# A third chunk's decays loaded earlier, and two more products ahead of the second pair's outputs, in a planned Mamba-2 plus expert-mixture kernel

## The chip, the cores and the metric

The kernel runs on one core of a Trainium2 chip. The metric is the device time of one execution in microseconds (us). Three executions of the kernel before took 616.87, 616.92 and 619.2 us, so its median is 616.92 us. The profile is of one execution, taken by the hardware profiler. Engine names follow the profile: PE is TensorE (matmul), PEld its weight load, DVE is VectorE, ACT is ScalarE, POOL is GpSimd, SP is SyncE, which here issues nearly all DMAs.

## The reference

The input is a state-space block followed by a mixture of four expert networks. There are 4 sequences of 768 positions, 8 heads, head size 32, state size 16.

```
# state space block, per batch and head, in chunks
L = exp(cum_i - cum_j), kept where i >= j       # cum: running sum of log(clip(a, 1e-6, 1))
y = ((C B^T) * L) x  +  C state * exp(cum)
state = exp(sum) * state + sum_j B_j x_j exp(cum_last - cum_j)
# bridge: x = y as [3072, 256]
# mixture of experts, e = 0..3, F = 1024
p = domain_probs / (row sum + 1e-9)
out += p[:, e] * (relu(x @ w1[e]) @ w2[e])
```

## The kernel before

The 3072 positions are cut into 24 chunks of 128; four chunks with the same place in their sequences follow one another. For each pair of chunks the kernel makes scores (L502, function `score`), multiplies them with a decay matrix into the tile MT on DVE (L856), and then makes the outputs of the pair and what they add to the state on PE (L546, function `inner`; with L879 for the share of the state of an earlier chunk, from the fifth chunk on). ACT copies the outputs away (L894) and keeps the state's part (L556).

For the first six chunks the decay matrix is made by scans on DVE (L519) into the tile LT. Chunks 0 to 2 get the decays spread over partitions by PE; from chunk 3 on they come from DRAM as a broadcast load (`load_decays`, L463) into one of two tiles `ab`. That load reads `acut_d`, a DRAM copy of the clipped decays with each first entry zeroed, which the kernel itself stores (`store_decays`, L630) after POOL has clipped the decays `a_sb` in place (L608), copied them (L626) and zeroed the first column (L627).

The expert networks take the products with the weights (L933, function `product`: one product is two matmuls of 128x256, and the trace has two records for each such matmul). Most of the work is done in schemes that save products by sums of blocks (L1024 for weights, L960, L1043 and L1260 for tokens and results). The first pair of chunks is done with plain products, four blocks of w1 (`plain_first`) and eight products for the second layer (`own_`, from `visit`); each second-layer product needs one gated result of DVE (L968) and one block of w2. The second pair begins with the products named `begun` and `ones`.

Two things set the order around the change. The first stage, up to about 13 us, is written out by hand in the order of the text: the loads on SP are issued in that order, by one sequencer that waits in place. Everything after it is a list of pieces of work. PE's order is the list `line`, written by hand; for DVE, ACT, POOL and SP a planner (`Plan.run`) simulates the engines with given costs and times at which tiles are ready (`plan.taken(..., now + x)`) and fixes their order before the kernel runs. The constants OWN, SCORED and LEFT say how many second-layer products of the first pair stand ahead of the second pair's outputs, ahead of the third pair's scores, and behind the third pair's outputs:

```
line.extend(own_[:OWN])
outputs([2, 3])
...
fill = own_[OWN:SCORED] + put(*[begun[two][0] for two in twos]) + ones + own_[SCORED:]
line.extend(fill[:SCORED - OWN])
scores([4, 5])
line.extend(fill[SCORED - OWN:len(fill) - LEFT])
outputs([4, 5])
line.extend(fill[len(fill) - LEFT:])
```

The names "second pair" and "third pair" below are chunks 2 and 3, and chunks 4 and 5.

Of the kernel before, what the change touches and what calls it, by code (L numbers as in the profile page):

```python
# [10 lines left out]
ALU = mybir.AluOpType  # L11
# [22 lines left out]
LEAN = 4.0  # L34
EASY = 40.0
SCANNED = 6
SCORED, OWN, LEAD, LEFT = 5, 2, 5, 3
FILLED = 3
HORIZON, OPENING, LOADED = 26.0, 80.0, 1.0
ORDERS = (0, 1, 2, 3), (3, 1, 2, 0), (0, 1, 2, 3), (3, 1, 2, 0)  # L40
# [319 lines left out]
def kernel(  # L360
# [10 lines left out]
    nc = tc.nc  # L371

    NCH, _, W = xbc.shape
# [19 lines left out]
    def real(c):  # L393
        return c % NSEQ * NC + c // NSEQ
# [5 lines left out]
    def turned(c):  # L400

        lo = P // NQ * turn_of(c) if c >= NSEQ else 0
        return [(lo, 0, P - lo), (0, P - lo, lo)][:1 + (lo > 0)]
# [17 lines left out]
    def some(n, shape, name, pool=const):  # L421
        return [pool.tile(shape, FP32, name=f"{name}{i}") for i in range(n)]

    homes = {
        "V": some(NV - 4, [P, 2, FB], "v"),
        "W": some(NW, [P, 2 * FB], "w"),
        "bank": some(8, [P, 512], "bank", psum),
        "xb": some(4, [P, W], "xb"),
        "ab": some(2, [P, NH * P], "ab"),
        "ah": some(3, [HN, P], "ah"),  # L430
        "MT": some(2, [P, 2, NH, P + N], "MT"),
        "ctm": some(4, [HN, NT, P], "ctm"),
# [14 lines left out]
    st = {c: {} for c in range(NCH)}  # L447
# [4 lines left out]
    def load_tokens(c, xb):  # L452
        src = xbc[real(c)]
        if len(turned(c)) > 1:
            nc.sync.dma_start(out=xb[:, :OBT], in_=src[:, :OBT])
            for there, here, n in turned(c):
                nc.sync.dma_start(out=xb[here:here + n, OBT:], in_=src[there:there + n, OBT:])
        else:
            nc.sync.dma_start(out=xb, in_=src)

    def load_decays(c, ab):
        src = acut_d if c < SCANNED else cum_d
        nc.sync.dma_start(  # L463
            out=ab, in_=src[real(c)].rearrange("h s -> (h s)").partition_broadcast(P))
# [10 lines left out]
    def load_w1(fb, w):  # L475
        e, f = divmod(fb, EPB)
        nc.sync.dma_start(
            out=w.rearrange("p (a f) -> p a f", a=2),
            in_=w1[e].rearrange("(a p) f -> p a f", a=2)[:, :, f * FB:f * FB + FB])

    def load_w2(fb, w):
        e, f = divmod(fb, EPB)
        nc.sync.dma_start(
            out=w.rearrange("p (j m) -> p j m", j=JJ),
            in_=w2[e, f * FB:f * FB + FB].rearrange("(j p) m -> p j m", p=P))
# [27 lines left out]
    def place(c, h):  # L513

        return (h + NH // 2) % NH if c >= NSEQ and c % 2 else h

    def scan(LT, src, lo):
        w = src.shape[1]
        nc.vector.tensor_tensor_scan(  # L519
            out=LT.rearrange("p h s -> p (h s)")[:, lo:lo + w], data0=src,  # L520
            data1=ident.rearrange("p h s -> p (h s)")[:, :w], initial=0.0,
            op0=ALU.mult, op1=ALU.add)

    def decay(c, MT, ab, neg, h):

        nc.scalar.activation(  # L526
            out=MT[:, place(c, h), 0:P], in_=ab[:, h * P:h * P + P], func=AF.Exp,
            bias=neg[:, h % NT, NQ * real(c) + h // NT:NQ * real(c) + h // NT + 1])
# [22 lines left out]
    def keep_state(c, A, y):  # L551
# [14 lines left out]
    a_sb = homes["cum"][0]  # L566
    a_cut = homes["V"][-4][:NCH * NH // 2, 0].rearrange("p (r s) -> p r s", r=2)
# [5 lines left out]
        out=aq0.rearrange("(q r) t s -> q r (t s)", q=NQ)[:, 0], in_=a_rows[:, 0])  # L573
    nc.scalar.dma_start(
        out=aq1.rearrange("(q r) c t s -> q r c (t s)", q=NQ)[:, 0], in_=a_rows[:, 1:SPREAD])
# [5 lines left out]
        out=a_sb, in_=a.rearrange("c h s -> (c h) s").rearrange("(p r) s -> p r s", r=2))  # L581
# [14 lines left out]
    for q in range(NQ):  # L596
        nc.vector.memset(tmask[32 * q:32 * q + N, 0:1], 1.0)
    nc.vector.tensor_scalar(out=tmask[:, 1:2], in0=tmask[:, 0:1], scalar1=-1.0, scalar2=1.0,
                            op0=ALU.mult, op1=ALU.add)
# [7 lines left out]
    def clip(engine, v, top=1.0):  # L607
        engine.tensor_scalar(out=v, in0=v, scalar1=1e-6, scalar2=top, op0=ALU.max, op1=ALU.min)  # L608
# [13 lines left out]
    clip(nc.vector, aq1.rearrange("p c t s -> p (c t s)"), own)  # L622
    nc.vector.memset(aq1[:, :, :, 0:1], 0.0)

    clip(nc.gpsimd, a_sb)
    nc.gpsimd.tensor_copy(a_cut, a_sb)  # L626
    nc.gpsimd.memset(a_cut[:, :, 0:1], 0.0)  # L627

    def store_decays(engine, d, sb):
        engine.dma_start(  # L630
            out=d.rearrange("c h s -> (c h) s").rearrange("(p r) s -> p r s", r=2), in_=sb)

    store_decays(nc.sync, acut_d, a_cut)
    load_tokens(3, xb[3])
    for fb in range(2, 4):
        load_w1(fb, homes["W"][fb])
    for fb in range(4):
        load_w2(fb, homes["W"][4 + fb])
    load_decays(3, homes["ab"][0])

    BANK = homes["bank"]
    rows = NCH * E
# [22 lines left out]
    def scan_quarters(c, LT, banks, part):  # L665
        for q in (2 * part, 2 * part + 1):
            scan(LT, banks[q][:, :NT * P], q * NT * P)
# [56 lines left out]
    for r in range(2):  # L724
        nc.vector.tensor_tensor_scan(
            out=sums[:, r], data0=a_sb[:, r], data1=zeros[:NCH * NH // 2], initial=0.0,
            op0=ALU.add, op1=ALU.add)
# [14 lines left out]
    plan = Plan(homes)  # L742
    line = []
    B512, B256 = {"DVE": D512, "POOL": 1.3}, {"DVE": D256, "POOL": .72}
    now = 13.2
# [9 lines left out]
    def act(us, fn, **kw):  # L755
        return plan.add({"ACT": us}, fn, **kw)

    def dve(us, fn, **kw):
        return plan.add({"DVE": us}, fn, **kw)
# [4 lines left out]
    def value(kind, **kw):  # L764
        return Value(kind, **kw)
# [8 lines left out]
    for c, i in ((2, 2), (3, 3)):  # L774
        st[c]["xb"] = plan.taken("xb", i, now)
    st[2]["ctm"] = plan.taken("ctm", 0, now)
    st[3]["ab"] = plan.taken("ab", 0, now + 2)
    for c in range(2):
        st[c]["A"] = plan.taken("A", c, now)
    g0 = gates[0, 0] = plan.taken("gate", 0, now)  # L780
# [18 lines left out]
    def decays(c):  # L799
        s = st[c]  # L800
        j = c % 2
        if not j:
            s["MT"] = st[c + 1]["MT"] = value("MT")
            s["made"] = st[c + 1]["made"] = []
        if c < SCANNED:
            for part in range(2):
                if c < SPREAD:
                    dve(1.2, lambda e, part=part: scan_quarters(
                        c, LT0[:, j], [b.t for b in s["a"]], part),
                        reads=s["a"][2 * part:2 * part + 2], part=LTv[2 * j:2 * j + 2])  # L810
                else:
                    half = NH * P // 2
                    dve(1.15, lambda e, lo=half * part: scan(
                        LT0[:, j], s["ab"].t[:, lo:lo + half], place(c, lo // P) * P), two=True,
                        reads=[s["ab"]], part=LTv[2 * j:2 * j + 2])
            plan.add({"POOL": .4}, lambda e: fade(
                c, s["MT"].t[:, j], s["xb"].t, LT0[:, j]),
                reads=[s["xb"], *LTv[2 * j:2 * j + 2]], part=[s["MT"]])
        else:
            made = {}  # L820
            for h in range(NH):
                made[h] = act(.38, lambda e, h=h: decay(
                    c, s["MT"].t[:, j], s["ab"].t, neg.t, h),
                    reads=[s["ab"], neg], part=[s["MT"]])
            cut = [plan.add({"POOL": .85}, lambda e, h=h: causal(
                s["MT"].t[:, j], place(c, h), NQ), part=[s["MT"]],
                behind=[made[x] for x in range(h, h + NQ)]) for h in range(0, NH, NQ)]
            s["made"] += cut
            if c < NCH - NSEQ:
                s["made"].append(plan.add({"POOL": .5 if place(c, 0) else .4}, lambda e: fade(  # L830
                    c, s["MT"].t[:, j], s["xb"].t, s["MT"].t[:, j]),
                    reads=[s["xb"]], part=[s["MT"]], behind=cut))
        if "ctm" not in s:
            s["ctm"] = value("ctm")
            act(.62, lambda e: mask(c, s["ctm"].t, s["xb"].t), reads=[s["xb"]], writes=[s["ctm"]])
        if c >= NSEQ:
            s["dec"], s["cts"] = value("dec"), value("cts")
            act(.3, lambda e: nc.scalar.activation(out=s["dec"].t, in_=s["ah"].t, func=AF.Exp),
                reads=[s["ah"]], writes=[s["dec"]])
            plan.add({"POOL": .72}, lambda e: nc.gpsimd.tensor_mul(  # L840
                s["cts"].t, s["ctm"].t, s["dec"].t.unsqueeze(1).to_broadcast([HN, NT, P])),
                reads=[s["ctm"], s["dec"]], writes=[s["cts"]])
# [503 lines left out]

    loaded = {}
    for fb in range(4):
        loaded[fb, 1] = plan.taken("W", fb, now + (0.0 if fb < 2 else 3.0))
        loaded[fb, 2] = plan.taken("W", 4 + fb, now + 4.0 + fb)  # L1350
    for (fb, l), v in loaded.items():
        weights["S", fb, l] = v

# [31 lines left out]
    for seq, _ in plain[2:]:  # L1385
        line.extend(seq)
    dma(lambda _: nc.sync.dma_start(
        out=g0.t[:, 4:6], in_=p_d[0, 4:6].rearrange("c s -> (c s)").partition_broadcast(P).rearrange(
            "p (c s) -> p c s", s=P)), kb=128, part=[g0])
# [7 lines left out]
    for c in (4, 5):  # L1397
        fetch(c)
        decays(c)
# [11 lines left out]
    made = [twos_first(two, begun[two]) for two in twos]  # L1411
# [48 lines left out]
    for u, (k, fbs) in enumerate(units):  # L1460
# [6 lines left out]
        seq, h = fours_first(k, fbs)  # L1467
# [96 lines left out]
```

## Time and profile before

| what | us |
|---|---|
| median of three executions | 616.92 (616.87 to 619.2) |
| span of the profiled execution, first to last instruction | 615.3 |
| PE busy | 605.7 (98%) |
| DVE busy | 489.5 (80%) |
| ACT busy | 292.5 (48%) |
| POOL busy | 157.6 (26%) |
| PE share of the chain that ended last | 92% |
| mean granted clock of PE | 0.997 |

For the profiled execution the span is what is given; against the median of the executions, 1.6 us (616.92 less 615.3) lie around it. The busy time of PE says how much of the span its records cover, not that each record ran at its best: a matmul of 128x256 has a record of 381 ns on average, while in a dense stretch, 24 records from 18.17 to 23.62 us, one starts every 0.227 us. Times within the span are counted from its start.

### The profile page before, as it was taken

How to read it: one execution, taken by the hardware profiler on the slowest of the kernel's cores; microseconds unless marked ns; L12 is line 12 of the kernel's file. 1: busy time of each engine (PE TensorE's matmuls, PEld its weight loads, DVE VectorE, ACT ScalarE, POOL GpSimd, SP SyncE). 2: the span in 40 equal slices, each digit the busy share in tenths (PEclk: the TensorE clock that was granted, in tenths of full speed). 3: DMA queues.
4: the chain of work that ended last, by engine and by line, in shares of the span. 5: the costliest groups of instructions: out<-in, count | busy, mean ns of one | idle time of the engine just before them, and what ended most of it. 6: DMA issues, size and time to landing. Idle time of an engine off the chain costs nothing.

```text
span 615.3 us, 10136 instructions
## 1 busy us (share of the span) xinstructions
PE 605.7 (98%) x3365; PEld 514.8 (84%) x3365; DVE 489.5 (80%) x854; ACT 292.5 (48%) x681; POOL 157.6 (26%) x238
## 2 busy tenths in 40 slices
PE   9899999999999999999999999999999999999997
PEld 5677878888888888888888888888888888888885
DVE  7879897998969895697978988386785979576775
ACT  4237646378651327877443333844444242434441
POOL 5536556636372000776500100210000000000000
PEclk9899999999999999999999999999999999999999
DMA  7737578676863429983442424964233232964001
GB/s 249 256 114 231 204 218 300 205 224 208 280 188 94 134 34 285 297 291 146 132 144 77 137 63 118 284 222 137 61 111 87 93 90 51 303 230 126 1 0 52
DMA packets 89060, 99.65 MB, mean 162 GB/s; under 512 B 27428, under 2 KB 58928, under 8 KB 89008
## 3 DMA queue, kind: packets, MB, share of 16 engines
q1 hardware_dynamic: 88852, 98.95, 51.4%
q8 instruction: 27, 0.44, 0.3%
q14 instruction: 25, 0.20, 0.1%
q10 hardware_dynamic: 156, 0.06, 0.0%
HBM read 78.80 MB, written 20.17 MB: 161 GB/s over the span
## 4 chain that ended last, share of the span: by engine, by line
PE 92%; DVE 2%; ACT 1%; issue 0%; DVEq 0%
PE bank L933 88%; PE bank L546 2%; PE bank L502 1%; PE bank L879 1%; DVE v L960 1%; DVE v L968 1%; ACT A L556 1%; DVE MT L856 0%; ACT v L894 0%; DVE bank L1071 0%; DVE v L1260 0%; PE bank L1325 0%; DVE v L1425 0%; ACT LT L894 0%; ACT v L1330 0%
## 5 line engine op out<-in xcount | busy, mean ns | idle before, releaser
L933 PE MATMUL bank<-v,w 128*128 128x256 f32 x1716 | 402.0, 381 | 1.1 <-DVE bank L1071 0.8
L933 PEld LDWEIGHTS bank<-v,w 128*128 128x128 f32 x1716 | 325.7, 191 | 50.0 <-issue 2.9
L933 PE MATMUL bank<-Y,w 128*128 128x256 f32 x692 | 177.3, 381 | 0.7 <-ACT LT L894 0.4
L933 PEld LDWEIGHTS bank<-Y,w 128*128 128x128 f32 x692 | 130.2, 190 | 21.9 <-issue 1.7
L1213 ACT COPY v<-bank 128x512 f32<-128x512 f32 x109 | 63.9, 586 | 177.5 <-PE bank L933 165.2
L968 DVE SCALAR_TENSOR_TENSOR v<-bank,gate 128x512 f32<-128x512 f32 x147 | 101.0, 688 | 39.6 <-PE bank L933 36.8
L960 DVE TENSOR_TENSOR v<-v,v 128x512 f32<-128x512 f32 x179 | 125.9, 720 | 2.1 <-ACT v L942 0.8
L1024 POOL TENSOR_TENSOR w<-w,w 128x256 f32<-128x256 f32 x94 | 72.1, 784 | 46.0 <-DVE v L960 13.8
L1071 DVE TENSOR_TENSOR bank<-bank,v 128x512 f32<-128x512 f32 x81 | 55.5, 696 | 35.2 <-PE bank L933 23.6
L942 ACT COPY v<-bank 128x512 f32<-128x512 f32 x97 | 56.7, 587 | 55.0 <-PE bank L933 46.7
L947 ACT COPY bank<-v 128x512 f32<-128x512 f32 x126 | 73.2, 594 | 10.8 <-DVE v L968 8.7
L526 ACT ACTIVATE MT<-ab,neg 128x128 f32<-128x128 f32 x144 | 46.9, 393 | 2.0 <-DMA ab<-cum_d 2.0
L933 PE MATMUL bank<-LT,w 128*128 128x256 f32 x168 | 42.6, 380 | 0.0
L531 POOL TENSOR_SCALAR_AFFINE_SELECT MT<-MT 128x512 f32<-128x512 f32 x36 | 23.0, 652 | 67.8 <-ACT MT L526 53.9
L933 PEld LDWEIGHTS bank<-LT,w 128*128 128x128 f32 x168 | 31.8, 190 | 4.6 <-DVE v L968 0.3
L1024 POOL TENSOR_TENSOR w<-w 128x256 f32<-128x256 f32 x32 | 24.2, 762 | 23.2 <-DVE Y L1043 9.0
L960 DVE TENSOR_TENSOR v<-bank,v 128x512 f32<-128x512 f32 x26 | 17.9, 689 | 11.7 <-PE bank L933 9.9
L1260 DVE TENSOR_TENSOR v<-v,v 128x256 f32<-128x256 f32 x58 | 22.9, 431 | 1.1 <-ACT v L1213 0.7
L856 DVE TENSOR_TENSOR MT<-bank,MT 128x512 f32<-128x512 f32 x36 | 22.7, 681 | 0.1
L968 DVE SCALAR_TENSOR_TENSOR v<-v,gate 128x512 f32<-128x512 f32 x26 | 19.7, 758 | 0.4
L1213 ACT COPY LT<-bank 128x512 f32<-128x512 f32 x12 | 7.0, 586 | 23.5 <-PE bank L933 23.5
L840 POOL TENSOR_TENSOR cts<-ctm,dec 128x256 f32<-128x256 f32 x20 | 14.5, 734 | 11.6 <-DVE v L960 5.1
(110 smaller groups left out, 322.1 us busy)
## 6 DMA issues: line engine op xcount, KB each, us to landing
w<-w_d SPq DMA_DIRECT2D x128, 256.0 KB
w_d<-w SPq DMA_DIRECT2D x64, 256.0 KB
w<-in_w_dram SPq DMA_DIRECT2D x40, 256.0 KB
ab<-cum_d SPq DMA_DIRECT2D x18, 512.0 KB
w<-in_w_dram SPq DMA_DIRECT2D x64, 128.0 KB
gate<-p_d SPq DMA_DIRECT2D x15, 384.0 KB
xb<-in_xbc_dram SPq DMA_DIRECT2D x17, 192.0 KB
out_dram<-v SPq DMA_DIRECT2D x144, 16.0 KB
```

Source lines behind the costliest of these rows:

```text
L526: nc.scalar.activation(out=MT[:, place(c, h), 0:P], in_=ab[:, h * P:h * P + P], func=AF.Exp, bias=neg[:, h % NT, NQ * real(c) + h // NT:NQ ...
L531: nc.gpsimd.affine_select(out=MT[:, h:h + n, 0:P], in_=MT[:, h:h + n, 0:P], compare_op=ALU.is_ge, fill=0.0, base=0, pattern=[[0, n], [1, P ...
L856: nc.vector.tensor_mul(to, g, LT0[:, js, h] if cs[0] < SCANNED else to)
L933: nc.tensor.matmul(out=o, lhsT=w[:, j], rhs=x if half is None else x[:, j], start=(start and j == 0), stop=(j == 1), skip_group_check=True)
L942: act(.5, lambda e: nc.scalar.copy(out=flat(v), in_=bank.t), reads=[bank], writes=[v])
L947: act(.54 if to - lo > FB else .32, lambda e: nc.scalar.copy(out=bank.t[:, lo:to], in_=flat(v)[:, lo:to]), reads=[v], writes=[bank])
L960: plan.add(engines, lambda e: (on(e).tensor_add if sign > 0 else on(e).tensor_sub)(flat(v), whole(x), whole(y)), reads=[x, y], writes=[v], ...
L968: dve(D512, lambda e: nc.vector.scalar_tensor_tensor(out=h.t, in0=whole(x).rearrange("p (j m) -> p j m", j=JJ), scalar=0.0, in1=g.t[:, 2 * ...
L1024: plan.add(B256, lambda e, r=r, x=x, y=y, sign=sign: (on(e).tensor_add if sign > 0 else on(e).tensor_sub)(view(r), view(x), view(y)), two= ...
L1071: dve(D512, lambda e: (nc.vector.tensor_add if sign > 0 else nc.vector.tensor_sub)(to.t, bank.t, whole(x)), reads=[x, bank], writes=[to])
L1213: act(.5, lambda e: nc.scalar.copy(out=flat(v), in_=bank.t), reads=[bank], writes=[v], hold=HOLD)
L1260: plan.add(engines, lambda e: (on(e).tensor_add if sign > 0 else on(e).tensor_sub)(o[1](), x[1](), y[1]()), reads=[v for v in vs if v is n ...
```

## The change

The decays' DRAM copy is made on another engine and stored a little earlier in the text: DVE clips `a_sb` straight into `a_cut` and zeroes its first column, and POOL clips `a_sb` in place after that, where it had clipped, copied and zeroed. The load of chunk 3's decays is issued ahead of the two w1 and four w2 loads instead of behind them. OWN goes from 2 to 4 and SCORED from 5 to 7 (LEFT stays 3). Three ready times and one cost that the planner reckons with are altered.

```diff
-SCORED, OWN, LEAD, LEFT = 5, 2, 5, 3
+SCORED, OWN, LEAD, LEFT = 7, 4, 5, 3
...
+    nc.vector.tensor_scalar(out=a_cut, in0=a_sb, scalar1=1e-6, scalar2=1.0, op0=ALU.max, op1=ALU.min)
+    nc.vector.memset(a_cut[:, :, 0:1], 0.0)
     clip(nc.gpsimd, a_sb)
-    nc.gpsimd.tensor_copy(a_cut, a_sb)
-    nc.gpsimd.memset(a_cut[:, :, 0:1], 0.0)
...
     store_decays(nc.sync, acut_d, a_cut)
     load_tokens(3, xb[3])
+    load_decays(3, homes["ab"][0])
     for fb in range(2, 4):
         load_w1(fb, homes["W"][fb])
     for fb in range(4):
         load_w2(fb, homes["W"][4 + fb])
-    load_decays(3, homes["ab"][0])
...
-    st[3]["ab"] = plan.taken("ab", 0, now + 2)
+    st[3]["ab"] = plan.taken("ab", 0, now + 2.5)
...
-                made[h] = act(.38, lambda e, h=h: decay(
+                made[h] = act(.30, lambda e, h=h: decay(
...
-        loaded[fb, 1] = plan.taken("W", fb, now + (0.0 if fb < 2 else 3.0))
-        loaded[fb, 2] = plan.taken("W", 4 + fb, now + 4.0 + fb)
+        loaded[fb, 1] = plan.taken("W", fb, now + (0.0 if fb < 2 else 4.0))
+        loaded[fb, 2] = plan.taken("W", 4 + fb, now + 6.0 + .8 * fb)
```

With LEFT at 3, what stands behind the third pair's outputs changes too. Before, three second-layer products of the first pair stood there; after, the two products `ones` and one of the first pair. Ahead of the second pair's outputs, between them and the third pair's scores, and between those scores and the third pair's outputs stood 2, 3 and 6 products; after the change it is 4, 3 and 4. On DVE the four MT products of the third pair follow each other, where two gated results had stood between them.

## The prediction

> **What bounds the kernel now.** I read the page first. PE is busy for 98% of the span and holds 92% of the chain that ended last, nearly all of it in the dense products L933. So time can only be won where PE stands still or runs slowly. PE's list of waits, longest first, tells where:
>
> ```profile
> PE 605.7 (98%) x3365; PEld 514.8 (84%) x3365; DVE 489.5 (80%) x854; ACT 292.5 (48%) x681; POOL 157.6 (26%) x238
> PEclk9899999999999999999999999999999999999999
> ...
> PE bank L546 <- POOL w L1024: 1.4, 1, 1.4
> PE bank L684 <- PEq L1556: 0.8, 1, 0.8
> PE bank L933 <- DVE bank L1071: 0.8, 1, 0.8
> PE bank L1325 <- DVE v L1260: 0.7, 1, 0.7
> PE bank L546 <- DVE MT L856: 0.7, 1, 0.7
> ```
>
> Two of the waits are at L546, the outputs of the second pair, and in the page's second slice of the clock an 8 stands: the only dip inside the span. PE's timeline and the table by stage show both:
>
> ```profile
> 18.17 5.45 PE L933 MATMUL bank<-v,w 128*128 128x256 f32 x24
> 24.98 0.41 PE L546 MATMUL bank<-MT,xb 128*32 128x144 f32 x2 [1.36 <-POOL w L1024]
> 26.08 1.18 PE L546 MATMUL bank<-MT,xb 128*32 128x144 f32 x30 [0.70 <-DVE MT L856]
> 27.19 4.54 PE L933 MATMUL bank<-v,w 128*128 128x256 f32 x12
> ...
> 25.38:27.39 2.01, 1.31 (x32) 1.00 0.87 273
> 27.39:30.80 3.41, 3.41 (x9) 0.50 0.60 228
> 30.80:38.50 7.70, 7.70 (x52) 1.00 0.11 39
> ```
>
> The reader is to see that 24 records of L933 take 5.45 us ahead of the wait (0.227 each), but 12 take 4.47 us behind it (chain: 27.26 to 31.73, 0.37 each): the column after the counts is the granted clock, and it is 0.50 from 27.39 to 30.80. The first wait is put down to POOL; by the chain of waits it was DVE, whose MT products ended at 24.83 and 26.04. So the third view is DVE's timeline:
>
> ```profile
> 16.56 0.67 DVE L968 SCALAR_TENSOR_TENSOR v<-bank,gate 128x512 f32<-128x512 f32 x1
> 19.13 1.23 DVE L519 TENSOR_TENSOR_SCAN LT<-ab,ident 128x512 f32<-128x512 f32 x1 [1.90 <-DMA ab<-acut_d]
> 20.27 0.67 DVE L968 SCALAR_TENSOR_TENSOR v<-bank,gate 128x512 f32<-128x512 f32 x1
> 20.85 1.39 DVE L519 TENSOR_TENSOR_SCAN LT<-ab,ident 128x512 f32<-128x512 f32 x1
> 25.34 0.68 DVE L856 TENSOR_TENSOR MT<-bank,LT 128x512 f32<-128x512 f32 x1
> ```
>
> DVE waits 1.90 us for chunk 3's decays and then works without a break until MT is done at 26.02.
>
> **What the stall costs.** PE ends its products at 23.62 and the outputs at 27.26: 3.64 us for 32 matmuls that take 1.12 us in the third pair (39.12 to 40.23 in the chain). That is 2.52 us lost. At half clock 12 records take 4.47 us, where 12 x 0.227 = 2.72: 1.75 us lost. Together **4.27 us**, the most that the change can win here; all other waits of PE between 30 and 600 us sum to about 1.8 us.
>
> **Two more products in front.** They are moved, not added: 2 products, 8 records, 8 x 0.227 = 1.82 us. PE reaches the outputs at 23.62 + 1.82 = 25.44. The products' inputs are there: the second gated result ended at 20.94, and PE asks for it at about 21.8.
>
> **The earlier load.** Of the store: DVE does the clip and the zeroing. By the neighbouring rows of the same lines (0.35 us for 128x256, 0.06) that is 0.41 us, and DVE is idle for 0.87 us there, from 4.48 to 5.35, waiting for PE; so it costs nothing; without that cover, 0.41. POOL's clip (1.07) starts some 0.4 us later and its copy and zeroing (0.49) go; its next work is at 8.05. SP then issues the store behind the token load at about 5.9, not 6.35. SP's rows:
>
> ```profile
> 6.35 0.34 SPq L630 DMA_DIRECT2D acut_d<-v  x1
> 6.73 0.43 SPq L459 DMA_DIRECT2D xb<-in_xbc_dram  x1
> 7.20 0.99 SPq L477 DMA_DIRECT2D w<-in_w_dram  x2
> 8.23 2.96 SPq L483 DMA_DIRECT2D w<-in_w_dram  x4
> 11.23 0.47 SPq L463 DMA_DIRECT2D ab<-acut_d  x1
> ```
>
> The load reads what the store writes, so **it adds a wait on SP**. When does the store land? The last w2 load, issued at 10.82, had waited 0.4 us for a token load issued ahead of the store, so that one landed at about 10.8. The decays' load went out at 11.23 without a wait, so the store had landed by then. Issued 0.45 us sooner behind the same loads it lands at about the same time, 10.8 to 11.2; if it does not queue, as soon as 8.1 (2.2 us after issue, as the first token load, 1.92, for which ACT waited until 4.25). I take 11.1, the row nearest to it. So the load is issued at 11.1, hardly sooner than now. What changes is its place: it no longer stands behind 1.5 MB of weights. Issue plus 2 us plus its bytes (0.5 MB, 1.5 us at the 350 GB/s of that stretch) gives 14.6, with a slower broadcast 15.6. DVE wants it at 17.23, when its gated result ends: the 1.90 us go. MT is done at 26.02 - 1.90, about 24.1, ahead of PE's 25.44 by 1.3 us. No wait is left there, nothing else comes late (POOL's share of MT, L540, follows the scan), and the clock stays up. If the load were no sooner at all, MT at 26.02 would leave 0.6 us.
>
> The Trainium skill, DMA: Bandwidth & Descriptors (Rules for kernel authors), says that a DMA which reads what an earlier one wrote must wait for that one's semaphore before it is issued, and its section on the anatomy of one DMA that the wait is on the issuing sequencer, with a fixed cost of about 2.0 us. By that figure alone the store would land at 8 us and SP would stand for 1 us, not 4; the sum is the same.
>
> **Who queues behind that wait.** SP stands from 6.7 to 11.1, and only one token load (0.3 MB) is in the queue then. The six weights are issued from 11.6 to 14.5 in place of 7.2 to 11.2, and the queue runs dry for about 1.5 us. With decays at 15.6 and 0.75 us per 0.26 MB, they land at 16.4, 17.1, 17.9, 18.6, 19.4 and 20.1. PE wants the third w1 block at 18.17, the fourth at 19.1, the first w2 block at 20.0, the second at 21.8. Cover: 1.8 us at the least; gone, PE waits one to one. Everything later on SP comes about 2 us later as well: tokens, heads and decays of chunks 4 and 5 (decays issued at 16.38 and 22.75 now, scanned from 26.11 and 30.05).
>
> **The new weak place** is the third pair. PE's count of products up to its outputs is 11 before and after, so PE gets to its MT at 39.12 - 4.27 = 34.85. DVE needs, from the rows of now: scans of chunk 4 2.83, two sums 1.26, scans of chunk 5 2.33, one sum 0.4, four MT 2.6. From 24.1 without a wait that is 33.5. If chunk 5's decays land at 30, it is 30 + 5.3 = 35.3: 0.5 us of wait. Bounds: nothing, and, if they come the full 2 us later than the 30.05 at which they are used now, 37.4, so 2.5 us. I take 0.5. In the stretch from 40 to 100 us, DVE is 90% busy and PE waits 0.33 + 0.80 + 0.43 = 1.56 us. PE comes 4 us sooner and the planner's orders differ; bounds 1.56 saved and 1.56 added; I take 0.3 lost, since DVE has little room.
>
> **Sum.** 4.27 - 0.5 - 0.3 = 3.5 us won. The profiled span of 615.3 would become 611.8; with the 1.6 us around it, from the median of 616.92, **613.4**.
>
> **The rivals.**
> - The wait moves on (0.17): chunk 5's decays land at 30.8 to 32, or the denser DVE stretch takes it back; 1.2 to 3 us lost: 614 to 616. For it: DMA rows above; against it: DMA is only 0.28 to 0.52 busy from 20 to 22 us, so the queue can catch up.
> - The load is no sooner (0.06), because the store or the broadcast takes until 19: 0.6 us more is left, 614.0.
> - The clock's dip isn't the stall's (0.07): only 2.52 is won, less 0.8: 615.2. Against it: it begins 1.3 us after PE restarts, lasts 3.41 us and doesn't come back for 580 us.
> - Slower (0.05), one mechanism: chunk 5's decays land after 32 us, so PE's wait at the third pair passes 2.5 us and the clock halves there too (1.75). At 33 us that is 3.5 + 1.75 + 0.3 lost against 4.27 won: 618.2. It decides from about 32.2.
>
> The third rival has a page behind it: the Trainium skill, TensorE: Matmul & The Clock Gate (the table of why this matters), warns of idle gaps over about 3 us. Here the two gaps sum to 2.06 us and the clock was 0.50 afterwards, so the row speaks for a shorter limit; by the page alone 1.75 us would stay.
>
> **How the numbers follow.** The forecast has 0.65, its own range 612.4 to 614.8. The range to hold 8 in 10 takes in most of the first three rivals above and a kept 1.56 below: 612.2 to 616.2. A measurement can tell 0.5%, here 3.1 us; faster by more means under 613.84. Of the forecast's 0.65 some 0.51 lies there, with 0.03 from the second rival: 0.54. Slower by more than that, over 620.0, needs over 7 us lost: 0.03. The rest, 0.43, is within 0.5%.
>
> **What would show it.** Right: no wait of PE at L546 near 25 us, granted clock 1.00 from 27 to 31, DVE's first scan of `ab` at about 17.2 without a wait, SP's load issued at about 11 after a wait for the store, the w1 and w2 loads behind it, third pair's outputs at about 35. Wrong: PE waits at L933 between 18 and 22 for weights, or over 1 us at L879 or L546 near 35, or a clock of 0.50 anywhere up to 600 us.

## The result, and the profile after

The changed kernel takes 614.0 us in the median of 22 executions (613.08 to 615.26). The kernel before, run beside it, takes 615.25 us (22 executions, 613.67 to 619.2, the three known ahead of the prediction among them). The ratio is 0.9977, with a 95% interval of 0.9966 to 0.9988: faster by 1.4 us, 0.7 to 2.1. Forecast were 613.4 us and 3.5 us less. On two other occasions the whole change gave ratios of 0.9984 (0.9972 to 0.9997) and 0.9992 (0.9980 to 1.0004); the last interval reaches past 1. In all three the change is under 0.5%.

The two profiled executions differ by more than the medians do: spans of 615.3 and 611.9 us, 3.4 us. That contrast is the subject of what follows. First the page of the changed kernel, busy time and granted clock:

```profile
PE 604.1 (99%) x3365; PEld 514.1 (84%) x3365; DVE 488.0 (80%) x856; ACT 292.5 (48%) x681; POOL 160.0 (26%) x236
...
PEclk9999999999999999999999999999999999999999
```

The 8 in the second slice of the clock is gone. PE's timeline (start, length, matmuls; in brackets the idle time before, and what ended it):

```profile
17.83 7.17 PE L933 MATMUL bank<-v,w 128*128 128x256 f32 x32
24.94 1.19 PE L546 MATMUL bank<-MT,xb 128*32 128x144 f32 x32
...
29.92 3.80 PE L933 MATMUL bank<-v,w 128*128 128x256 f32 x16
33.96 1.14 PE L879 MATMUL bank<-cts,S 32*32 32x256 f32 x16 [0.24 <-DVE MT L856]
35.03 1.21 PE L546 MATMUL bank<-MT,xb 128*32 128x144 f32 x32
```

The second pair's outputs (24.94) follow the products without a break. There is a new wait at the third pair, at L879. DVE's timeline says why:

```profile
16.81 1.22 DVE L519 TENSOR_TENSOR_SCAN LT<-ab,ident 128x512 f32<-128x512 f32 x1
...
24.41 2.40 DVE L519 TENSOR_TENSOR_SCAN LT<-ab,ident 128x512 f32<-128x512 f32 x2 [0.83 <-DMA ab<-acut_d]
...
29.96 2.34 DVE L519 TENSOR_TENSOR_SCAN LT<-ab,ident 128x512 f32<-128x512 f32 x2 [2.34 <-DMA ab<-acut_d]
```

Chunk 3's decays are there when DVE gets to them, as forecast; chunk 4's cost DVE 0.83 us and chunk 5's 2.34. SP's rows, and its longest wait, show where that comes from:

```profile
6.36 0.43 SPq L459 DMA_DIRECT2D xb<-in_xbc_dram  x1
10.93 0.33 SPq L463 DMA_DIRECT2D ab<-acut_d  x1
11.30 0.95 SPq L477 DMA_DIRECT2D w<-in_w_dram  x2
...
SPq L463 <- DMA acut_d<-v: 4.0, 1, 4.0
```

SP stands for 4.0 us until the store has landed, and the DMA queue runs dry meanwhile. In the table by stage, the last two columns are the DMA engines' busy share and GB/s:

```profile
9.00:10.00 1.00, 1.00 (x24) 0.51 (x20) 1.00 (x3) 0.43 (x2) 0.00 (x0) 1.00 1.00 384
10.00:11.00 1.00, 1.00 (x14) 0.94 (x8) 0.90 (x3) 0.46 (x2) 1.00 (x2) 1.00 0.31 118
11.00:12.00 1.00, 1.00 (x16) 0.62 (x17) 1.00 (x4) 0.59 (x1) 0.35 (x2) 1.00 0.10 36
```

Set matmul against matmul, PE's lead over the profile of before is 0.34 us at 13 us, 4.0 at 40 and at 100 us, 3.55 at 125 and 3.35 from 272 us to the end. The 0.34 us isn't the change's: some executions of the changed kernel have it and some don't (see the last section). So 3.0 us remain for the change. The sum of the prediction (3.5 forecast) nearly holds between these two executions, and still the medians are only 1.25 us apart.

### The profile page after: what moved, and what is told of

Read it like the earlier page. It is cut to its first block, busy times and chain, and to the rows that moved or that the text cites. A ratio compares the mean times of both kernels' runs of the same rounds, so it can differ in the third digit from the quotient of the medians.

```text
span 611.9 us, 10137 instructions
## 1 busy us (share of the span) xinstructions
PE 604.1 (99%) x3365; PEld 514.1 (84%) x3365; DVE 488.0 (80%) x856; ACT 292.5 (48%) x681; POOL 160.0 (26%) x236
## 4 chain that ended last, share of the span: by engine, by line
PE 91%; DMA 3%; DVE 2%; SPq 1%; ACT 1%; issue 1%; DVEq 0%
PE bank L933 87%; PE bank L546 2%; PE bank L502 1%; DMA cum_d<-cum 1%; DMA ab<-acut_d 1%; PE bank L879 1%; DMA acut_d<-v 1%; ACT A L556 1%; PE bank L684 1%; DVE v L960 1%; DVE v L968 0%; SPq L477 0%; DVE LT L519 0%; SPq L483 0%; DVE bank L1071 0%
## 5 line engine op out<-in xcount | busy, mean ns | idle before, releaser
L960 DVE TENSOR_TENSOR v<-v,v 128x512 f32<-128x512 f32 x175 | 122.2, 713 | 1.3
L1071 DVE TENSOR_TENSOR bank<-bank,v 128x512 f32<-128x512 f32 x84 | 57.5, 696 | 35.1 <-PE bank L933 21.9
L947 ACT COPY bank<-v 128x512 f32<-128x512 f32 (+1 forms) x124 | 72.2, 591 | 13.3 <-DVE v L968 9.9
L531 POOL TENSOR_SCALAR_AFFINE_SELECT MT<-MT 128x512 f32<-128x512 f32 x36 | 23.6, 671 | 64.2 <-ACT MT L526 55.1
L1260 DVE TENSOR_TENSOR v<-v,v 128x256 f32<-128x256 f32 x55 | 21.5, 428 | 0.6 <-ACT v L1213 0.3
L1213 ACT COPY LT<-bank 128x512 f32<-128x512 f32 x16 | 9.4, 586 | 25.2 <-PE bank L933 25.2
L495 ACT ACTIVATE ctm<-xb,tmask 128x128 f32<-128x128 f32 x48 | 15.7, 394 | 5.6 <-DMA xb<-in_xbc_dram 5.6
```

The lines of the kernel that those rows point to most:

```text
L531: nc.gpsimd.affine_select(out=MT[:, h:h + n, 0:P], in_=MT[:, h:h + n, 0:P], compare_op=ALU.is_ge, fill=0.0, base=0, pattern=[[0, n], [1, P ...
L947: act(.54 if to - lo > FB else .32, lambda e: nc.scalar.copy(out=bank.t[:, lo:to], in_=flat(v)[:, lo:to]), reads=[v], writes=[bank])
L960: plan.add(engines, lambda e: (on(e).tensor_add if sign > 0 else on(e).tensor_sub)(flat(v), whole(x), whole(y)), reads=[x, y], writes=[v], ...
L1071: dve(D512, lambda e: (nc.vector.tensor_add if sign > 0 else nc.vector.tensor_sub)(to.t, bank.t, whole(x)), reads=[x, bank], writes=[to])
L1213: act(.5, lambda e: nc.scalar.copy(out=flat(v), in_=bank.t), reads=[bank], writes=[v], hold=HOLD)
L1260: plan.add(engines, lambda e: (on(e).tensor_add if sign > 0 else on(e).tensor_sub)(o[1](), x[1](), y[1]()), reads=[v for v in vs if v is n ...
```

## The experiments

**Theory A**: the half clock behind the stall belongs to some executions of the kernel before, because it depends on how the stall falls into a window that keeps its own time; the profile of before showed one of these. **Rival B**: it is in every execution and something else shifts the times. Beside this: which part of the change wins, and whether the new wait at the third pair comes from SP standing for the store. The expectations of the later runs count this last idea to theory A as well. Medians below are of the executions of one kernel on one chip, with the kernel before run in between.

**1. The kernel before, again** (no edit).

> The kernel before, once more, so that each of its executions is listed with its span and its granted clock. Theory A: the half clock behind the stall at the second pair's outputs is there in some executions only, since the stall is as long as the window that decides and the window's start shifts; then executions near 615.2 us have a mean clock of 0.999 or more, and those near 617 us one of about 0.997, and the first are the more frequent. Rival B: the half clock is in every execution and something else shifts the times; then all have a clock of about 0.997.

Measured: 615.14 us in the median of 12. Of the 95 executions of the kernel before, on this and two later occasions, that are listed with their clock, 71 have a mean clock of 0.998 or more, at 613.5 to 615.9 us, median 614.8. The other 24 have 0.994 to 0.997, at 616.5 to 618.6, median 617.0. Nothing lies between. The second profile of the same kernel, PE's timeline:

```profile
24.97 0.40 PE L546 MATMUL bank<-MT,xb 128*32 128x144 f32 x2 [1.36 <-POOL w L1024]
26.07 1.18 PE L546 MATMUL bank<-MT,xb 128*32 128x144 f32 x30 [0.70 <-DVE MT L856]
27.18 2.86 PE L933 MATMUL bank<-v,w 128*128 128x256 f32 x12
```

and its table by stage (PE, granted clock, DMA share, GB/s):

```profile
27.40:30.80 3.40, 3.40 (x28) 1.00 0.46 174
```

The stall is the same to 0.01 us, 1.36 and 0.70. But the 12 records behind it take 2.86 us where they took 4.54, the clock stays at 1.00, and PE is ahead of the first profile by 1.70 us from there to the end. Theory A holds in that only some executions have the half clock (on what it depends, see run 11): one in four pays the 1.7 us, and the three times known ahead of the prediction (616.87, 616.92, 619.2) all lie on that side, as only 3 of the 19 others of the result do.

**2. The earlier load alone**, with the product counts and planner's numbers of before:

```diff
+    nc.vector.tensor_scalar(out=a_cut, in0=a_sb, scalar1=1e-6, scalar2=1.0, op0=ALU.max, op1=ALU.min)
+    nc.vector.memset(a_cut[:, :, 0:1], 0.0)
     clip(nc.gpsimd, a_sb)
...
+    load_decays(3, homes["ab"][0])
     for fb in range(2, 4):
...
-    load_decays(3, homes["ab"][0])
```

> The earlier load and store alone, with 2 and 5 products and the planner's numbers of before. Theory A: MT of the second pair is done at about 23.6 to 24.1 us, PE stands there for about 0.6 us instead of 2.06, the clock stays up, and the third pair, whose decays come about 2 us later, makes PE wait some 1.2 us at about 35 us; together some 0.5 to 1 us faster than before in the median. Rival: the load was what mattered, and this is as fast as the whole change (ratio 0.998).

Measured: 617.29 us, ratio 1.0027 (1.0009 to 1.0045): slower than before, against both expectations. PE's timeline, at the third pair:

```profile
24.34 1.18 PE L546 MATMUL bank<-MT,xb 128*32 128x144 f32 x30 [0.36 <-DVE MT L856]
...
34.91 1.99 PE L933 MATMUL bank<-v,w 128*128 128x256 f32 x8 [1.80 <-DVE v L968]
```

The wait moves, almost whole, from the second pair (0.36 left) to the third: DVE's scans of chunk 5 start at 30.40 after 2.02 us of waiting for their decays, and a gated result behind them is late. This profiled execution has full clock, and 1.65 us of lead over the first profile of before; 8 of the 12 executions have 0.994 to 0.997. The four with full clock have a median of 615.19 us, against 614.85 for those of before on this chip (23 of 35). So most of the loss is the half clock, which has become more frequent.

**3. The products alone**: the whole change, with the load behind the six weights again.

```diff
-    load_decays(3, homes["ab"][0])
     for fb in range(2, 4):
...
+    load_decays(3, homes["ab"][0])
```

> The whole change, but with the decays' load behind the six weights again. Theory A: MT of the second pair is done at about 25.7 us against PE's 24.9, so PE waits 0.7 us there with the clock up; the third pair's decays come as early as before, so no wait there. Within 0.5 us of the whole change, on either side. Rival: without the earlier load the stall and the half clock stay in part, 1 us or more slower than the whole change.

Measured: 613.66 us (613.37 to 614.3), ratio 0.9972 (0.9959 to 0.9986). DVE waits 2.35 us for chunk 3's decays, longer than before, and PE 0.46 + 0.10 us at the outputs; in all, its next products start at 27.08, 1.03 us later than in the first profile of the whole change (26.05). No execution has a clock under 0.999. That is 0.6 us below the whole change on the same chip (614.29, run 4), a little outside the 0.5 expected: the products are worth as much as the whole change or more. The kernel also keeps the store made on DVE and the new planner numbers, but its load goes out at 11.55 us, no sooner than before (11.23), and runs 9 and 10 find the new numbers the slower ones.

**4. The whole change, again.**

> The whole change once more, on the same chip as the others: ratio 0.9977, executions from 613.1 to 615.3 us, all with a clock of 0.998 or more. A second profile shows whether the wait at the third pair (0.24 us in the first) changes from one execution to the next, as it should if the arrival of the decays for chunks 4 and 5 is what spreads the times.

Measured: 614.29 us (613.11 to 615.56), ratio 0.9984. All 12 executions have 0.999 or 1.000, so their spread of 2.4 us isn't the clock's. In the profile, chunk 5's scans begin at 29.94 after a wait of 2.47 us.

**5. The load behind four weights**: the whole change, with

```diff
-    load_decays(3, homes["ab"][0])
     for fb in range(2, 4):
         load_w1(fb, homes["W"][fb])
-    for fb in range(4):
+    for fb in range(2):
         load_w2(fb, homes["W"][4 + fb])
+    load_decays(3, homes["ab"][0])
+    for fb in range(2, 4):
+        load_w2(fb, homes["W"][4 + fb])
```

> The whole change, but the decays' load stands behind two w1 and two w2 loads instead of ahead of all six. SP reaches it at about 10.4 us, when the store has nearly landed, so SP hardly waits and the queue does not run dry. Theory A: the decays land at about 17.5 us, MT of the second pair is done by about 24.5 against PE's 24.9, chunk 5's decays come as early as before, so PE waits neither at the second nor at the third pair: 613.2 to 613.6 us in the median, executions within 1 us of each other, 0.3 to 1 us faster than the whole change. Rival: the spread of the whole change comes from elsewhere, and this one has the same median and the same spread of 2.4 us.

Measured: 612.94 us (612.73 to 613.63), ratio 0.9974 (0.9964 to 0.9984): 1.5 us below the whole change on the same chip (614.49, run 8), more than the 0.3 to 1 us expected. PE's timeline:

```profile
24.96 1.19 PE L546 MATMUL bank<-MT,xb 128*32 128x144 f32 x32
...
33.67 0.66 PE L881 MATMUL bank<-cts,S 32*32 32x256 f32 x16
```

and DVE's:

```profile
18.02 1.23 DVE L519 TENSOR_TENSOR_SCAN LT<-ab,ident 128x512 f32<-128x512 f32 x1 [1.09 <-DMA ab<-acut_d]
...
29.04 2.34 DVE L519 TENSOR_TENSOR_SCAN LT<-ab,ident 128x512 f32<-128x512 f32 x2 [0.49 <-DMA ab<-acut_d]
```

The load goes out at 10.95 us as in the whole change, for the store lands no sooner, but four weights are on their way by then and SP stands for 1.6 us only. DVE waits 1.09 us for chunk 3, which the two products cover, and PE waits at neither pair (16 records of L879, here L881, in 0.66 us). The spread is 0.9 us instead of 2.4.

**6. The load behind two weights** (as in 5, but directly behind the two w1 loads).

> The whole change, but the load stands behind the two w1 loads. SP still waits for the store, for about 2.5 us instead of 3.9, and the queue holds 0.5 MB more meanwhile. Theory A: between the whole change and the load behind four weights, in the median and in the spread. Rival: no difference from the whole change.

Measured: 613.64 us (612.67 to 614.36), ratio 0.9972 (0.9960 to 0.9985). SP's wait is 2.5 us and DVE's for chunk 5 1.90: between the two in each, as theory A has it.

**7. The stall filled with work**: the kernel before, with

```diff
             vs = {}
+            for _ in range(2 if cs[0] == 2 else 0):
+                idle(ys[cs[0]].t)
             for c in cs:
```

> The kernel before, with two matmuls of 128x512 on constants put on PE right ahead of the second pair's outputs, into the bank that these overwrite: 1.7 us of PE work whose result nobody reads, in place of waiting. MT comes as late as before. Theory A: the clock stays up in every execution, none is near 617 us, and the median is that of the executions of before with full clock, 614.8, though its work is more. Rival: the half clock has another cause and some third of the executions keep a clock of 0.997 or less.

Measured: 614.88 us (614.19 to 615.81), ratio 0.9997 (0.9985 to 1.0010); 11 executions, all with 0.998 or more. Of before on the same chip, 6 of 31 are lower; at that rate 2 of 11 would be, and none with a chance of one in ten. PE's timeline:

```profile
23.46 1.89 PE L684 MATMUL bank<-const-float32-1.0 128*128 128x512 f32 x4
25.27 1.19 PE L546 MATMUL bank<-MT,xb 128*32 128x144 f32 x32
```

Useless work in the stall's place leaves the time as it is and removes the executions near 617: this speaks for the stall as the cause of the half clock, in a small number of executions. The kernels with two more products in front, in which the stall is gone or 1 us long, say the same: of their 96 executions (the result and runs 3 to 6, 8 to 10 and 12) none has a clock under 0.998. In this profiled execution chunk 3's decays were scanned from 17.51 on, after 0.27 us of wait, against 19.13 in both profiles of before, with the same order on SP (the load went out at 10.71 us here, at 11.23 and 11.02 there). So the landing of that load moves by 1.6 us between executions, and with it the stall; that would be a reason for the range of 613.5 to 615.9 us within full clock, but no profile of the two ends was had.

**8. The whole change, a third time.**

> The whole change on the same chip as the other three: 613.1 to 615.6 us, median 614.0 to 614.3, clock 0.998 or more. By theory A it is the slowest of the three that differ in the load's place, and the most spread.

Measured: 614.49 us (613.0 to 615.76), ratio 0.9992. Against 5 and 6 the order is as expected, 614.49, 613.64 and 612.94, and so is that of the ranges, 2.8, 1.7 and 0.9 us.

**9 and 10. The planner's numbers of before**, in kernel 5, beside kernel 5 once more:

```diff
-    st[3]["ab"] = plan.taken("ab", 0, now + 2.5)
+    st[3]["ab"] = plan.taken("ab", 0, now + 2)
...
-                made[h] = act(.30, lambda e, h=h: decay(
+                made[h] = act(.38, lambda e, h=h: decay(
...
-        loaded[fb, 1] = plan.taken("W", fb, now + (0.0 if fb < 2 else 4.0))
-        loaded[fb, 2] = plan.taken("W", 4 + fb, now + 6.0 + .8 * fb)
+        loaded[fb, 1] = plan.taken("W", fb, now + (0.0 if fb < 2 else 3.0))
+        loaded[fb, 2] = plan.taken("W", 4 + fb, now + 4.0 + fb)
```

> The whole change with the load behind four weights, but with the ready times and the cost of before given to the planner. PE's lead over the kernel before shrinks from 4.0 us at 40 us to 3.4 at 270 us in the changed kernel's profile. If the planner's new order (set by those numbers) loses it, the lead stays near 4 us here and the median is about 0.6 us lower; if the order is that of the changed product counts, or the stretch has no room for more lead, nothing changes beyond 0.3 us.

> The whole change with the load behind four weights, once more, to stand beside the kernel with the old planner numbers on one chip: median 612.7 to 613.1 us, executions within 1 us, clock 0.998 or more.

Measured: 612.67 us (612.48 to 613.4) with the old numbers, ratio 0.9960 (0.9944 to 0.9976), and 613.09 (612.55 to 613.54) with the new ones. The executions overlap, but the profiles part where the changed kernel lost its lead over before; PE's waits with the old numbers

```profile
PE bank L935 <- DVE bank L1073: 0.7, 1, 0.7
PE bank L935 <- ACT LT L896: 0.4, 1, 0.4
```

and with the new ones

```profile
PE bank L935 <- DVE bank L1073: 0.9, 2, 0.7
PE bank L935 <- ACT LT L896: 0.4, 1, 0.4
PE bank L935 <- DVE v L970: 0.3, 1, 0.3
PE bank L935 <- ACT v L896: 0.2, 1, 0.2
```

Between 64 and 270 us PE loses 0.65 us against the kernel with the old numbers (ahead by 0.10 at 64 us, behind by 0.55 from 270 us to the end). So the new order costs about half a microsecond. The fastest kernel of the study has the products, the load behind four weights and the old numbers.

**11. The earlier load alone, one execution more.**

> The earlier load and store alone, a second look at one execution. Eight of twelve executions had a mean clock of 0.997 or 0.994. If the half clock follows the new wait of 1.8 us at 33 us, an execution with 0.997 shows a clock of 0.50 for 3.4 us that begins between 34 and 38 us; if it is the old stall's, it begins near 27. An execution with full clock shows neither and has a span near 613.6.

Measured: 617.11 us, clock 0.996. The half clock is at neither of the places expected. PE's timeline and the table by stage:

```profile
29.40 2.41 PE L502 MATMUL bank<-ctm,xb 32*128 32x256 f32 x16 [1.53 <-ACT A L556]
...
30.80:34.20 3.40, 3.40 (x16) 2.30 (x10) 2.94 (x4) 0.34 (x1) 0.14 (x1) 0.52 0.36 136
```

In this execution PE waited 1.53 us at the third pair's scores, for ACT, and the clock halved from 30.7 us on, 1.3 us after PE went on, as in the first profile of before. The loads behind the early one were later still (scans of chunk 5 at 31.26, not 30.40). So a single wait of 1.5 us can do it, and in run 2 one of 1.8 us did not.

The traces say more about this. In each of the fourteen, every later change of the granted clock lies a whole number of 3.413 us after the place where the clock first went up: 6 and 7 such stretches for the two half clocks, 177 or 178 for the fall at the kernel's end. Cut at these places, PE's time shows how much of a stretch each wait took up:

| trace | stretch (us) | PE busy | PE idle | clock in the next stretch |
|---|---|---|---|---|
| before | 23.98 to 27.39 | 1.72 | 1.69 | 0.50 |
| run 11 | 27.24 to 30.66 | 1.82 | 1.60 | 0.50 |
| run 1 | 22.25 to 25.66 | 1.76 | 1.65 | 1.00 |
| run 1 | 25.66 to 29.08 | 3.01 | 0.41 | 1.00 |
| run 2 | 30.15 to 33.56 | 2.96 | 0.45 | 1.00 |
| run 2 | 33.56 to 36.97 | 2.06 | 1.35 | 1.00 |

The wait of 1.8 us in run 2 is cut in two, 0.45 and 1.35; the one of run 11 lies whole in one stretch. So the place of a wait among the stretches matters beside its length. The stall of before is cut differently in its two profiles, but in both it takes up nearly half of one stretch; why 1.69 us halved the clock and 1.65 us did not is not shown.

**12. The whole change, one execution more.**

> The whole change, a fourth look at one execution. If the arrival of chunk 5's decays spreads its times, the scans of chunk 5 begin at another time than 29.9 or 30.6 us where the span is another than 611.8 to 612.7, and PE's start behind the third pair's outputs (36.2, 36.2 and 36.8 us so far) moves with it one to one.

Measured: 614.37 us, span 612.7. In the four profiles the scans of chunk 5 begin at 29.96, 29.94, 30.60 and 30.71 us, and PE starts its products behind the third pair's outputs at 36.17, 36.15, 36.82 and 36.93: 6.21 to 6.22 us later each time. The arrival of chunk 5's decays sets the third pair one to one, as expected. Executions near 615.5 us weren't caught in a profile; that they have the same wait, longer, is inferred from run 5.

## Why the prediction was right and wrong

**Failed: the 1.75 us of half clock, counted whole.** "Together 4.27 us, the most that the change can win here" took the profiled execution for the usual one, and the median of three, 616.92, agreed with it. A quarter of the executions have that clock (24 of 95), and it moves their median by 0.2 us only (614.97 of all, 614.78 of the 71). So the base was about 614.8 to 615.25, not 616.92, and a gain of 1.25 us was measured where 3.5 was forecast.

The larger chance, 0.54, stood on a gain of over 0.5%; what came lies within 0.5%, which had 0.43. The predicted time, 613.4, is still only 0.6 below the measured one, since the same half clock stood in the base and in the gain: 616.92 less 1.75 is 615.17, near the measured 615.25. The 0.6 is about what the two terms that were taken too small (below) fall short by. One of the signs of being right, a clock of 1.00 from 27 to 31 us, tells little, for the kernel before shows it too (run 1).

The third rival, "the clock's dip isn't the stall's", fell: run 7 lost the dip with the stall's idle time, and so did the changed kernels. But its consequence, that only 2.52 us are to be won, held for most executions for another reason that the prediction did not name.

The Trainium skill, TensorE: Matmul & The Clock Gate (Part 1: The HAM clock gate), says that the window is 3413 ns long and free-running, so that runs of one kernel differ. The traces agree: the half clock lasted 3.41 us in both profiles that show it, it started 20.48 and 23.89 us after the clock had gone up (6 and 7 such windows), and the same 2.06 us of stall had it once and once not. The clock first went up 3.79 to 6.91 us after the start, so the windows fall differently in each execution. The prediction weighed the limit for an idle gap that the same page of the Trainium skill gives and left out this sentence, which bore on the sum.

**Right: the stall of 2.52 us.** It went, and no wait is left at the second pair in four profiles of the changed kernel. **Right in kind, not in credit:** MT was done at 23.6 us (24.1 forecast) and PE came at 24.9 (25.44), but the margin of 1.3 us was not needed: run 3, without the early load, loses 1.03 us there and is no slower in the median, since it loses nothing at the third pair.

**Right: what SP's wait does.** The load went out at 10.93 us (11.1 forecast), after 4.0 us of waiting, with the weights issued from 11.30 to 14.5 and the queue nearly empty for 1.5 us or more. PE waited for no weight, as forecast. By the fixed cost of 2.0 us that the prediction took from the Trainium skill, DMA: Bandwidth & Descriptors (the anatomy of one DMA), the store would have landed at 8 us; the rows say 10.9. (That section is about DMAs issued by GpSimd; this store is issued by SP.) That the store queues behind the loads issued ahead of it fits this, but no run separates it from other reasons.

**Mis-sized: the wait at the third pair**, taken at 0.5. From the start of the 16 records of the begun products to the next products took 6.25, 6.18, 6.56 and 6.68 us in the four profiles of the whole change and 5.44 in run 5: 0.7 to 1.2 us, within the bounds of 0 and 2.5 that were given. Chunk 5's scans were forecast for 30 and began at 29.9 to 30.7; and PE can be there sooner than the forecast 34.85, at 34.27 in run 5. The first rival ("the wait moves on") describes the early load, if not the whole change. **Mis-sized: 0.3 for the later stretch**: PE's lead fell by 0.65 us, none of it between 40 and 100 us, where the prediction expected it, and in run 9 against 10 the planner's numbers account for about as much.

With these sizes the sum is 2.5 less 0.7 to 1.2 less 0.65, so 0.6 to 1.1 us, for an execution with full clock and the stall of the two profiles, and 1.7 more for one in four. Between executions with full clock on one chip, the medians are 0.55 us apart in run 4 (614.85 to 614.29) and 0.3 in run 8 (614.80 to 614.49); the stall of before is shorter in some of them, if run 7's early landing is no exception. The 1.25 between the medians of the result holds some of the rarer executions too.

Two small slips of the working change nothing: from 1.92 to 4.25 us is 2.3 us, not 2.2, and by its own terms the fourth rival is slower than before from about 32.05 us on, not 32.2.

## What to carry to other kernels

One profile and three times can all lie on the rarer side of something that only some executions have; a dip of the clock that is one window long is such a thing, so its price is to be counted by how often it occurs. By runs 5, 6 and 8, a load that waits for a store belongs in its queue at the place where the store has landed: put ahead of other loads it stops them all, and the wait it saves comes back two stages later. Moving ready work in front of a stall was worth the whole gain here, and hides late loads of any cause.

## What the runs showed of the hardware that was not expected

- Idle stretches of 1.53 us (run 11) and of 1.36 and 0.70 us close together (the first profile of before) were followed by half clock for 3.41 us; the latter, to 0.01 us the same, were not in run 1, nor was one of 1.80 us in run 2. By the table under run 11, what counts is how much of one stretch of 3.413 us is idle, about half: 1.60 and 1.69 us were followed by half clock, 1.65 us was not. At the kernel's end 1.81 us (run 6) was and 1.74 us (run 8) was not. PE's idle time alone does not put these in order, so the exact limit stays open.
- PE's first hand-written stage ends 0.34 us sooner in the profiles in which the clock went up 3.8 to 4.6 us after the start than in those where it did at 5.2 us or later: PE starts the second pair's scores at 16.75 to 16.81 us in the first and at 17.09 to 17.10 in the others, whichever kernel it was. This is part of the 3.4 us between the two first profiles.
- A store of 96 KB that was issued at 5.97 us behind loads still in flight let its reader go at 10.93 us, and the same broadcast load of 512 KB, issued in the same place, was awaited until 19.13, 19.13 and 17.51 us in three executions (issued at 11.23, 11.02 and 10.71).
